# Chunk 0's keys in runs of 16 tokens, its lengths on GpSimd, its diagonal blocks from PSUM, and unread products moved into the joins

## The chip, the cores and the metric

The kernel runs on one core of a Trainium2 chip. The metric is the device time of one execution in microseconds. A core has five engines with instruction queues of their own: TensorE (PE for its products, PEld for its weight loads), VectorE (DVE), ScalarE (ACT), GpSimd (POOL) and SyncE (SP), which here only issues transfers. The tensors lie in HBM, the engines work in SBUF (128 partitions), and TensorE writes to the banks of PSUM.

## The reference

A delta-rule attention over 768 tokens for 4 x 8 heads of 48 channels, whose output goes through a feed-forward block with SiLU:

```python
q, k, v: (4, 8, 768, 48); beta: (4, 8, 768); w_in: (384, 2048); w_out: (2048, 384)
k_n = k / (np.linalg.norm(k, axis=-1, keepdims=True) + 1e-06)
for t in range(S):
    y[:, :, t] = np.einsum('bhd,bhde->bhe', q[:, :, t], state)
    v_old = np.einsum('bhde,bhd->bhe', state, kt)          # kt, vt, bt: token t
    state = state + bt[:, :, :, None] * np.einsum('bhd,bhe->bhde', kt, vt - v_old)
x = y.transpose(0, 2, 1, 3).reshape(B * S, H * D)
h = x @ w_in
out = (h * (1.0 / (1.0 + np.exp(-h)))) @ w_out
```

The keys are divided by their lengths. All is float32.

## The kernel before

The 768 tokens are six chunks of 128. Within a chunk the recurrence becomes algebra. The products of the chunk's keys with each other (the scores, `ap`) are scaled by a step for each token and head (minus beta over the square of the length), and a triangular matrix of 32 x 32 blocks is inverted: first the diagonal blocks, by a chain of small VectorE operations, then the blocks are joined by small TensorE products. The values times that inverse give `z`, and from `z` come the chunk's outputs and the update of the state. The outputs, turned into `xT`, run through the feed-forward block in half chunks.

Chunk 0 has nothing to hide behind, and the change concerns its opening. In the order of the program:

- `load_k(0)`: six transfers on SP bring the keys to `kbufs[0]` (`kb` in the profile), 48 floats of one token and head at a time, padded to 64. The padding is zeroed by VectorE. Beta comes by six transfers on ScalarE's queue, then the queries of chunk 0 (`z`'s buffer) on SP.
- `busy(n)` (L340 to L352) puts `n` products on TensorE whose result is never read, 384 wide: three at the start, four behind the first query turns, two behind the betas, six within the inversion.
- Lengths: GpSimd squares the keys (L385), VectorE adds (L389), and `norm_steps(0)` (L391 on) does the reciprocal square root by three rounds of small VectorE operations, then the step of each token and turns it (L426).
- `turn(0, b, 0, ...)` transposes the keys by TensorE (L510) and `first_score(b)` makes the scores of batch row `b` (L539), which ScalarE and VectorE copy to `ap`.
- `diagonal_blocks(0, g, ...)` copies the 32 x 32 blocks on the diagonal from `ap` to `stage`, eight copies by GpSimd and ScalarE, and `turn_diagonal(0)` (L578) turns them on VectorE.
- `invert_first` is the chain: scale by the step (L697), fifteen rounds of L705 and L709, two turns (L716, L720).
- `joins(0)` joins the blocks: `corner` (L743, its sums on VectorE at L750), `turned` (L759), `straight` (L772) and `merge_half` (L832), for each of two groups of batch rows (`g`). The list `between` says what is put behind each of the ten stages: `fill(1)` and `begin_next()` are steps that narrow the weights to the form that the feed-forward block uses (L233, L234 on ScalarE, L238, L242 on VectorE, L246 on GpSimd).
- Then `inner` (L866), `first_outputs` (L910), and the first feed-forward products (`phid`, L1088). From there a script of letters sets the order, with the second half of the chunk and the next chunks threaded between feed-forward products.

Each engine takes its instructions in program order (`pin` ties each to the one before). SP's transfers are in one line (`in_line`). Transfers of later weights are released by counts of TensorE instructions (`loads`): the first two, in `fetch_w_in(2)` and `(3)`, within `turned` and `straight`.

## Time and profile before

| | |
|---|---|
| median of 3 runs | 634.13 us (633.98 to 637.14) |
| the profiled execution | 633.96 us |
| its span in the profile | 631.8 us |
| TensorE busy | 617.7 us (98%) |
| VectorE / ScalarE / GpSimd busy | 415.5 / 226.7 / 94.0 us |
| mean granted TensorE clock over the span | 0.989 |

The profile is of one execution. Times in it count from the span's start; what lies around the span is 2.2 us. A row of the timeline gives start, length, engine, line, operation, output and input, and in brackets how long the engine had been idle and what ended that. A row of the groups ends with the busy time and the mean length in ns, then the idle time ahead of it. A row of a stretch gives its length and then, for PE, PEld, DVE, ACT and POOL, the busy time with the number of instructions, and last the granted clock, the share of the DMA engines and GB/s. "issue" is a wait for nothing that the profile shows.

### The profile page before, as it was taken

To read this page: it belongs to the slowest core of one execution; us is meant where nothing else is said; L and a number is where in the kernel's file an instruction comes from. 1 tells how busy PE (TensorE), PEld (TensorE's weight loads), DVE (VectorE), ACT (ScalarE), POOL (GpSimd) and SP (SyncE) were. 2 spreads that over 40 slices of the span, in tenths; PEclk is the share of its full clock that TensorE was granted. 3 is DMA by queue.
4 is the path that set the end of the run, shared out by engine and by line. 5 is a ranking of instruction groups with operands and counts; after the bars stand their busy time and mean duration, and the time that the engine had idled before them with its cause. 6 is when DMAs were issued, how large, how long until landed. Compare 5 with 4: busy or idle time off the path is not lost.

```text
span 631.8 us, 21374 instructions
## 1 busy us (share of the span) xinstructions
PE 617.7 (98%) x9390; PEld 543.3 (86%) x9390; DVE 415.5 (66%) x927; ACT 226.7 (36%) x516; POOL 94.0 (15%) x101
## 2 busy tenths in 40 slices
PE   8889989999999999999999999999999999999997
PEld 5578778666799989989989989989989989988997
DVE  6886779999667974546975554976444983345432
ACT  4657873332441122451122451122452122454210
POOL 5234631335020020020020010020002000000000
PEclk9869999999999999999999999999999999999999
DMA  9656506350459360459141359433254024010011
GB/s 175 134 141 199 170 16 149 116 86 4 101 100 186 62 108 4 95 107 188 34 92 20 72 125 156 65 75 44 52 113 95 2 75 62 17 38 1 0 26 26
DMA packets 136941, 52.61 MB, mean 83 GB/s; under 512 B 108672, under 2 KB 130432, under 8 KB 136848
## 3 DMA queue, kind: packets, MB, share of 16 engines
q1 hardware_dynamic: 136512, 51.09, 39.6%
q8 instruction: 74, 1.21, 0.9%
q10 hardware_dynamic: 336, 0.15, 0.1%
q14 instruction: 19, 0.16, 0.1%
HBM read 39.09 MB, written 9.96 MB: 78 GB/s over the span
## 4 chain that ended last, share of the span: by engine, by line
PE 93%; SPq 2%; DMA 1%; issue 1%; ACT 1%; DVE 0%
PE phid L1088 34%; PE px L1200 17%; PE py L1200 13%; PE po L1132 5%; PE pb_c L866 3%; PE pa L539 2%; SPq L144 2%; PE pb_c L1303 2%; PE pb_c L854 2%; PE pyc L945 2%; PE pc L1303 2%; PE pb_c L1132 2%; PE pb_c L886 2%; PE pa L1303 1%; PE pyc L932 1%; PE px L808 1%
## 5 line engine op out<-in xcount | busy, mean ns | idle before, releaser
L1088 PE MATMUL phid<-xT,w_in 128*128 128x256 f32 x960 | 214.9, 382 | 1.9 <-issue 1.7
L1088 PEld LDWEIGHTS phid<-xT,w_in 128*128 128x128 f32 x960 | 180.2, 190 | 26.9 <-issue 2.8
L1098 ACT ACTIVATE gT<-phid 128x512 f32<-128x512 f32 x72 | 42.9, 597 | 115.2 <-PE phid L1088 106.2
L656 DVE SCALAR_TENSOR_TENSOR rank<-g,step,x 128x31 f32<-128x31 f32 (+15 forms) x124 | 49.8, 402 | 23.3 <-DMA g<-blocks 19.8
L1200 PE MATMUL px<-sums_of_w,sums_of_g 128*128 128x192 f32 x320 | 56.6, 329 | 0.0
L1200 PE MATMUL py<-w_out,sums_of_g 128*128 128x192 f32 x320 | 56.2, 328 | 0.0
L1200 PEld LDWEIGHTS px<-sums_of_w,sums_of_g 128*128 128x128 f32 x320 | 52.2, 190 | 0.4
L1200 PEld LDWEIGHTS py<-w_out,sums_of_g 128*128 128x128 f32 x320 | 52.3, 190 | 0.3
L661 DVE TENSOR_TENSOR x<-x,rank 128x31 f32<-128x31 f32 (+15 forms) x124 | 42.5, 342 | 4.3
L477 POOL TENSOR_TENSOR vf<-vf,n_slot 128x768 f32<-128x768 f32 x10 | 14.8, 1492 | 175.4 <-DMA vf<-in_v_dram 129.9
L1183 DVE TENSOR_TENSOR sums_of_g<-gT 128x384 f32<-128x384 f32 (+1 forms) x48 | 24.6, 540 | 14.6 <-ACT gT L1098 14.5
L498 DVE STREAM_TRANSPOSE kq<-stage 128x512 f32<-128x512 f32 x28 | 28.4, 1121 | 6.8 <-DMA stage<-in_q_dram 3.5
L554 ACT COPY xT<-pyc 48x128 f32<-48x128 f32 (+2 forms) x120 | 31.1, 259 | 1.6
L1211 DVE TENSOR_TENSOR o<-o,kept 128x192 f32<-128x192 f32 (+1 forms) x29 | 11.5, 425 | 26.7 <-ACT kept L1208 26.7
L560 POOL COPY g<-x 64x256 f32<-64x256 f32 x4 | 5.0, 1244 | 150.8 <-DVE x L664 150.8
L891 DVE TENSOR_TENSOR state<-state,pb_c 128x384 f32<-128x384 f32 x22 | 11.2, 550 | 24.6 <-PE pb_c L886 24.6
L866 PEld LDWEIGHTS pb_c<-vf,xi 64*64 64x64 f32 x736 | 23.3, 138 | 3.2 <-issue 2.3
L866 PE MATMUL pb_c<-vf,xi 64*64 64x48 f32 x736 | 24.9, 223 | 0.1
L1132 PE MATMUL po<-w_out,gT 128*128 128x384 f32 x64 | 23.7, 491 | 0.0
L1200 PE MATMUL py<-w_out,gT 128*128 128x192 f32 x128 | 23.4, 331 | 0.0
L859 DVE TENSOR_TENSOR vf<-vf,pb_c 128x384 f32<-128x384 f32 x22 | 11.2, 550 | 18.3 <-PE pb_c L854 15.5
L1200 PE MATMUL px<-w_out,gT 128*128 128x192 f32 x128 | 22.4, 327 | 0.0
(293 smaller groups left out, 1094.5 us busy)
## 6 DMA issues: line engine op xcount, KB each, us to landing
vf<-in_v_dram SPq DMA_DIRECT2D x48, 96.0 KB, 2.8
out_dram<-o SPq DMA_DIRECT2D x42, 96.0 KB, 2.2
w_out<-in_moe_w_in_dram SPq DMA_DIRECT2D x4, 768.0 KB, 5.0
sums_of_w<-in_moe_w_out_dram SPq DMA_DIRECT2D x4, 768.0 KB, 4.6
kb<-in_k_dram SPq DMA_DIRECT2D x12, 192.0 KB, 4.5
kb<-in_k_dram SPq DMA_DIRECT2D x24, 96.0 KB, 4.0
raw<-in_moe_w_in_dram SPq DMA_DIRECT2D x3, 768.0 KB, 6.8
blocks<-ap SPq DMA_DIRECT2D x32, 64.0 KB, 1.9
```

Source lines behind the costliest of these rows:

```text
L477: pin(nc.gpsimd.tensor_tensor(out=vf, in0=vf, in1=of, op=ALU.mult))
L498: pin(nc.vector.transpose(out=kqs[c, b][:, :, j, :].rearrange("p a (i m) -> p a m i", i=T), in_=src.rearrange("p a (m d) -> p a m d", d=D) ...
L554: return pin(nc.scalar.copy(to, of))
L656: pin(nc.vector.scalar_tensor_tensor(out=tv, in0=g[:, 0:m, m : m + 1].to_broadcast([P, m, n]), scalar=step[:, m : m + 1], in1=x[:, m : m + ...
L661: yield pin(nc.vector.tensor_tensor(out=x[:, 0:m, m:T], in0=x[:, 0:m, m:T], in1=tv, op=ALU.add))
L866: yield pin(nc.tensor.matmul(pz[rows, n * D : (n + 1) * D], lhsT=xis[g][rows, u * H + 2 * p + e, :], rhs=vfs[c][rows, hf, g * HB + u, p, : ...
L1088: pin(nc.tensor.matmul(ph[:, j * GT : (j + 1) * GT], lhsT=w_in[:, a, (2 * f + j) * P : (2 * f + j + 1) * P], rhs=xTs[c, hf][:, a, :], star ...
L1098: pin(nc.scalar.activation(out=hidden_of(c, hf, f), in_=ph[:], func=ACTF.Silu, scale=-0.5 if in_blocks(c) else 0.5))
L1132: pin(nc.tensor.matmul(pos[i][:, 0:DM], lhsT=hidden_of(0, hf, f // 2)[:, at : at + C], rhs=w_outs[f // HFF][:, f % HFF, :], start=(f == 0) ...
L1183: pin(nc.vector.tensor_tensor(out=sums_of_g[:, k, fs], in0=of[0], in1=of[1], op=op))
L1200: pin(nc.tensor.matmul(to, lhsT=at, rhs=quarter(f, *b) if isinstance(b, tuple) else sums_of_w[b][:, f], start=start and f == 0, stop=f == ...
L1303: pin(nc.tensor.matmul(to[:, i * GT : (i + 1) * GT], lhsT=left(a, slice(f, f + 1))[:, 0], rhs=right(b), start=start and i == 0 and n == 0, ...
```

## The change

Chunk 0's keys come a second way. Two transfers bring them to `stage` (`keys_0`), for even and for odd heads; partition p holds 16 tokens in a row of one head, 3 KB in one piece. ScalarE and VectorE pad them into `kbufs[0]` (`pad`), TensorE turns them four steps at a time (`first_turn`), and a rearranged `turned_kq` takes them. The squares are made by ScalarE and GpSimd in two halves, the sums by VectorE; since tokens now lie along the free axis, four products with a selector matrix `sel` (built by VectorE from the identity) bring the sums to the tokens' partitions. GpSimd then does the reciprocal square root in fourteen small operations (`first_step`). The scores of a whole group stay in two PSUM banks; the diagonal blocks are taken from there by ScalarE and VectorE with the masks `halves`, and copied to `ap` afterwards. `load_k(0)` in its old form comes later, behind the values, for the update of the state. Half of beta's transfers move to SP. Unread products: three at the start with zeros as weights, then one 512 wide in two places, one 384 wide in two places within the inversion, and four 512 wide in the joins (`kept`).

```diff
-    for g in range(2):
-        load_k(0, slice(HB * g, HB * (g + 1)))
+    for e in range(2):
+        issue(
+            keys_0[:, e],
+            k.rearrange("b (a e) (c i s) d -> e c (b a) i (s d)", e=2, c=NCH, i=2 * NB)[e, 0],
+        )
...
+    def first_step():
+        po = bank(M, "po")
+        for i in range(2):
+            for e in range(2):
+                pin(nc.tensor.matmul(
+                    po[:, STEPS * i : STEPS * (i + 1)], lhsT=sel[:, e, i].rearrange("p j g n f -> p (j g n f)"),
+                    rhs=ss_0[:, e], start=e == 0, stop=e == 1,
+                ))
...
+        pin(nc.scalar.copy(ss, po[:, 0:T]))
+        pool, root = nc.gpsimd, seed.bitcast(FP32)
...
+        plus(n, u, None, 1e-6)
+        product(n_2, n, n)
+        yield
+        step_of[0] = small.tile([P, T], FP32, name="step")
+        pin(nc.vector.reciprocal(out=r, in_=n_2))
+        pin(nc.vector.scalar_tensor_tensor(
+            out=step_of[0][:], in0=r, scalar=-1.0, in1=stage[:, BH * T : BH * T + T], op0=ALU.mult, op1=ALU.mult
+        ))
+        pin(nc.scalar.copy(blocks[0][2].rearrange("p s t -> p (s t)")[:, 0 : T * T : T + 1], step_of[0][:]))
...
+    def first_score(g):
...
+        for e in range(2):
+            of = pa[e][:].rearrange("p (n t) -> p n t", t=W)
+            to = diagonals[0][:, HH * g + e : HH * (g + 1) : 2]
+            pin(nc.scalar.mul(to, of[:, :, 0:T], halves[:, 0:1]))
+            pin(nc.vector.scalar_tensor_tensor(
+                out=to, in0=of[:, :, T:W], scalar=halves[:, 1:2], in1=to, op0=ALU.mult, op1=ALU.add
+            ))
...
     load_v(0)
+    load_k(0)
     for b in range(2):
         turn(0, b, 1, M)
-    busy(4)
-    for _ in norm_steps(0):
-        pass
+    busy(1, wide=HB * NP * W)
+    next(steps)
...
-        if n in (9, 11, 13):
-            busy(2 if n < 13 else 1, done, Sync)
+        if n in (12, 14):
+            busy(1, done, Sync)
...
+    def kept():
+        busy(1, wide=HB * NP * W)
+
     together(joins(0, [
         lambda: (size_half(0, pins[seen_on]), begin_next(),),
-        lambda: (),
+        kept,
         lambda: (),
         lambda: (fill(1), fill(1),),
-        lambda: (fill(1),),
+        lambda: (fill(1), kept()),
         lambda: (),
-        lambda: (fill(1),),
-        lambda: (fill(1), begin_next(),),
+        lambda: (fill(1), kept()),
+        lambda: (fill(1), begin_next(), kept()),
```

On VectorE, around the turn of chunk 0's diagonals (`sums_of_w<-stage`), before: `n` and `nr`, `nt` are the lengths and what comes of them, `rank` the inversion's scratch.

```order
L417 TENSOR_TENSOR nt<-nr,ss 128x32
L418 TENSOR_SCALAR n<-nt 128x32
L419 RECIPROCAL nr<-n 128x32
L420 TENSOR_TENSOR nt<-nr,beta_tok 128x32
L423 SCALAR_TENSOR_TENSOR nt<-nr,nt 128x32
L426 STREAM_TRANSPOSE step<-nt 128x32
L578 STREAM_TRANSPOSE sums_of_w<-stage 128x32x32
L697 TENSOR_TENSOR sums_of_w<-sums_of_w,step 128x2x16x16
```

On VectorE at the same place, now: `pa` and `pb_c` are the PSUM banks with the scores.

```order
L447 TENSOR_REDUCE ss<-sq 128x2x8 x2
L1622 STREAM_TRANSPOSE stage<-beta_tok 128x32
L1597 SCALAR_TENSOR_TENSOR stage<-pa_232,halves,stage 128x8x32
L1597 SCALAR_TENSOR_TENSOR stage<-pb_c_73,halves,stage 128x8x32
L1597 SCALAR_TENSOR_TENSOR stage<-pa_271,halves,stage 128x8x32
L1597 SCALAR_TENSOR_TENSOR stage<-pb_c_74,halves,stage 128x8x32
L712 STREAM_TRANSPOSE sums_of_w<-stage 128x32x32
L508 RECIPROCAL nr<-seed 128x32
L509 SCALAR_TENSOR_TENSOR step<-nr,stage 128x32
L831 TENSOR_TENSOR sums_of_w<-sums_of_w,step 128x2x16x16
```

The root's sixteen steps have left VectorE; the diagonals come from PSUM in four steps, and the reciprocal and the step stand behind the turn.

On TensorE, from the second chunk's key turns (`pt<-ident,kb`) within the inversion to the first corner products (`ap`), before: `pb_c<-state,ident` are unread products.

```order
L347 MATMUL pb_c_74<-state_90,ident 128x384
L347 MATMUL pb_c_75<-state_90,ident 128x384
L510 MATMUL pt<-ident,kb_77 128x128 x4
L347 MATMUL pb_c_73<-state_90,ident 128x384
L347 MATMUL pb_c_74<-state_90,ident 128x384
L743 MATMUL pl<-sums_of_w,ap_168 32x16 x2
```

On TensorE at the same place, now, and then the end of the corners with the start of `turned` (L893):

```order
L643 MATMUL pt<-ident,kb_77 128x128 x12
L376 MATMUL pb_c_75<-state_96,ident 128x384
L643 MATMUL pt<-ident,kb_77 128x128 x4
L376 MATMUL pb_c_73<-state_96,ident 128x384
L877 MATMUL pl<-sums_of_w,ap_230 32x16 x2
...
L877 MATMUL pl<-sums_of_w,ap_269 32x16 x2
L376 MATMUL pb_c_73<-state_96,ident 128x512
L893 MATMUL pl<-sums_of_w 32x32
```

Of six unread products within the inversion two are left, and the first of the four kept ones stands between the corners and `turned`.

On SP, from the values (`vf`) to the queries of chunk 1 (`sums_of_g`), before: `w_out` takes raw parts of `moe_w_in`.

```order
L292 DMA raw<-in_moe_w_in_dram 128x3x512
L198 DMA vf<-in_v_dram 64x8x48 x8
L292 DMA w_out_109<-in_moe_w_in_dram 128x3x512 x2
L144 DMA sums_of_g<-in_q_dram 128x8x48
L144 DMA sums_of_g<-in_q_dram 64x8x48 x2
```

On SP at the same place, now:

```order
L303 DMA raw<-in_moe_w_in_dram 128x3x512
L198 DMA vf<-in_v_dram 64x8x48 x8
L144 DMA kb_76<-in_k_dram 128x8x48
L144 DMA kb_76<-in_k_dram 64x8x48 x2
L144 DMA kb_76<-in_k_dram 128x8x48
L144 DMA kb_76<-in_k_dram 64x8x48 x2
L303 DMA w_out_115<-in_moe_w_in_dram 128x3x512 x2
```

The six transfers of chunk 0's keys, which stood first on SP, now stand between the values and the next weights.

More of the change, by code (lines that the diff above doesn't have):

```diff
@@ L314 @@
     pin(nc.gpsimd.memset(states[0][:], 0.0))
+    zeros = states[0][:].rearrange("p u a w -> p (u a w)")
+    for _ in range(3):
+        done = pin(nc.tensor.matmul(
+            bank(CC, "pw")[:, 0:DM], lhsT=zeros[:, 0:P], rhs=zeros[:, 0:DM], start=True, stop=True
+        ))
+        tensor.append(done.ins.engine)
     make_identity(nc, ident[:])
@@ L1483 @@
     load_v(0)
+    load_k(0)
     for b in range(2):
         turn(0, b, 1, M)
[L1486 to L1488 removed]
+    busy(1, wide=HB * NP * W)
+    next(steps)
     first_queries(0)
```

189 lines of the change are left out of this document (144 added, 45 removed).

## The prediction

> **What bounds the kernel now.** First the page, for TensorE's share, then the busy time of each engine by stage: from 16.5 us (the lengths end on VectorE) to 31.2 (the joins begin), to 49.3 (the first product of the feed-forward), and the long rest from 92.
>
> ```profile
> PE 617.7 (98%) x9390; PEld 543.3 (86%) x9390; DVE 415.5 (66%) x927; ACT 226.7 (36%) x516; POOL 94.0 (15%) x101
> ...
> q8 instruction: 74, 1.21, 0.9%
> ...
> 16.50:31.20 14.70, 13.01 (x177) 8.77 (x179) 13.20 (x35) 9.28 (x24) 2.93 (x6) 0.88 0.69 138
> 31.20:49.30 18.10, 15.53 (x721) 14.61 (x721) 14.23 (x28) 10.20 (x22) 6.42 (x4) 0.72 0.53 135
> ...
> 92.00:631.80 539.80, 535.54 (x7240) 477.57 (x7240) 346.76 (x765) 165.00 (x391) 53.61 (x47) 1.00 0.37 73
> ```
>
> After each stage's length stand the busy times of PE, PEld, DVE, ACT and POOL with their counts, then TensorE's granted clock. From 92 us TensorE works 535.54 of 539.80 us; the change touches nothing there. So its worth is how much earlier the first feed-forward product (49.31) comes. Ahead of it PE's busy share flatters: much of it is unread products, and from 31.2 to 49.3 the clock is 0.72, which makes some 10 of the 18.1 us run at half.
>
> The opening hangs on one chain, seen in the order of time on VectorE, with ScalarE's and SP's rows that feed it:
>
> ```profile
> 2.65 0.48 DVE L208 MEMSET sums_of_g<- 128x512 f32 x1
> 15.45 0.35 DVE L419 RECIPROCAL nr<-n 128x32 f32<-128x32 f32 x1
> 16.18 0.19 DVE L423 SCALAR_TENSOR_TENSOR nt<-nr,nt 128x32 f32<-128x32 f32 x1
> 16.40 0.21 DVE L426 STREAM_TRANSPOSE step<-nt 128x32 f32<-128x32 f32 x1
> 16.54 1.98 DVE L578 STREAM_TRANSPOSE sums_of_w<-stage 128x1024 f32<-128x1024 f32 x1
> 18.55 0.69 DVE L697 TENSOR_TENSOR sums_of_w<-sums_of_w,step 128x512 f32<-128x512 f32 x1
> 28.01 1.06 DVE L716 STREAM_TRANSPOSE sums_of_w<-sums_of_w 128x512 f32<-128x512 f32 x1
> 28.92 1.95 DVE L720 STREAM_TRANSPOSE sums_of_w<-sums_of_w 128x1024 f32<-128x1024 f32 x1
> 31.92 0.34 DVE L750 SCALAR_TENSOR_TENSOR sums_of_w<-pl,second,pick 64x128 f32<-64x128 f32 x1 [1.05 <-PE pb_c L743]
> 12.30 3.75 ACT L554 COPY stage<-ap 32x512 f32<-32x512 f32 x6
> 6.23 1.61 POOL L385 TENSOR_TENSOR sq<-kb 128x384 f32<-128x384 f32 x2 [1.95 <-DMA kb<-in_k_dram]
> 9.00 1.61 POOL L385 TENSOR_TENSOR sq<-kb 128x384 f32<-128x384 f32 x2 [1.15 <-DMA kb<-in_k_dram]
> 33.12 4.36 SPq L292 DMA_DIRECT2D w_out<-in_moe_w_in_dram  x2
> 49.31 0.45 PE L1088 MATMUL phid<-xT,w_in 128*128 128x256 f32 x1 [0.15 <-DVE xT L919]
> ```
>
> The second half of the keys arrives at 9.00. The turn of the diagonals (L578, 16.54) then waits for two things that end together: the lengths on VectorE (their last step, L426, ends at 16.61) and ScalarE's copies of the diagonals (12.30 to 16.05). From there VectorE runs without a gap to 30.87, and then waits 1.05 us for the corners (L743).
>
> **Term 1, the turn of the diagonals comes earlier.** The rows for its parts:
>
> ```profile
> 1.00:2.00 1.00, 0.00 (x0) 0.00 (x0) 0.99 (x4) 0.00 (x0) 0.97 (x4) 1.00 0.10 27
> 13.00:14.00 1.00, 1.00 (x4) 0.57 (x3) 0.86 (x5) 0.99 (x2) 0.00 (x0) 1.00 1.01 369
> 16.72:17.92 1.20, 1.20 (x65) 1.13 (x66) 1.20 (x1) 0.89 (x3) 1.17 (x3) 1.00 0.92 162
> 9.12 1.06 PE L510 MATMUL pt<-ident,kb 128*128 128x128 f32 x8
> L522 DVE COPY kq<-pt 128x512 f32<-128x512 f32 x2 | 1.4, 686 | 0.2 <-PE pt L510 0.2
> L557 DVE COPY z<-pb_c 128x384 f32<-128x384 f32 x1 | 0.6, 560 | 0.0
> L389 DVE TENSOR_REDUCE ss<-sq 128x8 f32<-128x384 f32 x4 | 2.2, 545 | 2.6 <-POOL sq L385 2.6
> L557 DVE COPY ap<-pb_c 128x256 f32<-128x256 f32 x4 | 1.7, 425 | 0.5 <-PE pb_c L539 0.4
> L554 ACT COPY ap<-pa 128x256 f32<-128x256 f32 x8 | 3.0, 378 | 1.0 <-PE pb_c L539 0.8
> L1493 POOL COPY sums_of_w<-step 128x32 f32<-128x32 f32 x1 | 0.2, 249 | 0.1
> L1496 POOL MEMSET xi<- 128x1024 f32 x2 | 1.8, 955 | 0.0
> ```
>
> Keys: 0.786 MB in 3 KB runs. Bytes start to flow near 1.9 us; the weights, in 2 KB runs, flow at 369 GB/s in the second row, against 162 in the third, where 192-byte rows move. So 1.9 + 0.786/0.369 = 4.0 us at best, 6.8 at 162 GB/s, 9.0 as now. VectorE comes to the padding behind its memsets (over at 3.1, as now) and the 12 small copies that build the selector (at 0.19, as L423): 5.4; copies this small may follow each other closer, so I start the padding at 5.3. Two copies of 384 by VectorE, 2 x 0.5: 6.3. A small reduction (0.2) and a key copy (0.69): 7.2. Two sums of 768, each twice 0.545: 9.4; the squares on GpSimd (1.61 from 6.3) hide under that, and so do the transposes (0.53 for four). The four selector products and ScalarE's copy 0.6: 10.0. TensorE does 32 score products in 1.2 us (65 records in the third row), two groups: 12.4. After the last group ScalarE scales twice (2 x 0.38), VectorE adds behind it (0.42): 13.6. So the turn starts at **13.6 instead of 16.54**, -2.9; bounds 12.7 (keys and selector early) to 15.6 (keys at 6.8, half a us more in the copies).
>
> Lengths on GpSimd: its squares end near 8, three memsets of 0.95 follow, 10.8; then 14 small operations at 0.25 (the 128x32 copy; bounds 0.2 and 0.4, half a 384 product): 14.3, by bounds 13.6 to 16.4. They are needed when the turn is done, 13.6 + 2.0 = 15.6. Covered by 1.3 us, short by 0.8 at the upper bound.
>
> Behind the turn VectorE now does the reciprocal and the step (0.35 + 0.19, with gaps 0.65), and ahead of the corner sums one small transpose (0.21). The 16 steps are unchanged, 18.55 to 30.87. So the corner sums could start at 13.6 + 1.98 + 0.65 + 12.32 + 0.21 = 28.8, against 31.92: **-3.1**. The corner products must keep up. Now they do not:
>
> ```profile
> 28.21 1.29 PE pb_c L347 x4
> 31.16 0.20 PE L743 MATMUL pl<-sums_of_w,ap 32*32 32x16 f32 x2
> ```
>
> The corners' operand is turned at 29.07 (L716), yet they start at 31.16: the line that stands ahead of them on TensorE is the unread product (1.29 us for two, 0.645 each). The new order leaves two there instead of six, so the corners are ready in time, if the clock holds.
>
> **Term 2, joins to first product.** From 31.92 to 49.31 are 17.39 us, 10 of them at half clock. TensorE's waits and its instruction counts name a second limit:
>
> ```profile
> 32.49:35.90 3.41, 2.15 (x133) 1.81 (x132) 2.91 (x8) 1.45 (x4) 1.48 (x1) 0.98 0.44 108
> 35.90:39.31 3.41, 2.43 (x127) 2.29 (x128) 3.26 (x7) 1.88 (x5) 1.83 (x1) 0.50 0.59 178
> PE px L832 <- issue: 1.1, 1, 1.1
> PE py L832 <- issue: 1.1, 1, 1.1
> 35.92:39.48 3.56, 2.43 (x127) 2.29 (x128) 3.41 (x7) 2.04 (x5) 1.83 (x1) 0.50 0.62 183
> 35.93:49.31 13.38, 12.09 (x459) 11.51 (x460) 10.76 (x20) 7.69 (x16) 3.74 (x2) 0.62 0.60 154
> ```
>
> TensorE stops twice for 1.1 us with nothing to wait for, before 35.93 and before 39.49, and between the two restarts lie 127 + 128 = 255 instructions. All its 18780 instructions over the 74 packets (1.21 MB) of its instruction queue q8 give 254 each. So I read the stops as waits for the next packet: at best 256 instructions per 3.56 us here. From 35.93 to 49.31 are 919 instructions, 3.6 packets, 12.8 us if supply alone counts. Full clock can therefore gain little: 13.38 - 12.4 (three packets, 10.7, then the last products and two copies of 0.5, near 1.7) = 1.0. The four kept products (512 wide: 512/384 of 0.645 is 0.86 each, 3.4 together) fall into the same waits and I cost them at nothing; uncovered they cost 3.4. **-1.0**, bounds -2.7 (supply no limit) and +2.4.
>
> [...]
>
> **Moved transfers.** Six key transfers now stand between the values and the next weights on SP. SP idled from 26.30 to 33.12 there. Values end some 2 us earlier; six issues take 4.9 us at the values' rate (6.51 for eight) and 7.5 at the second keys', so SP is free between 29 and 32, and the weights' turn comes near 30. Cost 0; at the long end they come 2 us late, ScalarE's narrowing waits, and the last two join copies behind it.
>
> ```profile
> 19.79 6.51 SPq L198 DMA_DIRECT2D vf<-in_v_dram  x8
> 10.64 7.50 SPq L144 DMA_DIRECT2D kb<-in_k_dram  x6
> ```
>
> **Sum.** -3.1 - 1.0 = -4.1 on the profiled execution's 633.96: 629.9. The median shown is 634.13, 0.17 above it; I forecast **629.9**.
>
> **Rivals.** *Half clock from the corners on* (slower). The clock halved at 35.9 after a stretch in which TensorE was busy 2.15 of 3.41 us with 32-row products. Fifteen unread products ran ahead of the joins; now seven do, three of them before 4 us. If the clock falls before the corners, near 27 us, what ran at full clock from 31.16 to 35.9 (some 3.5 us of work) takes 3.5 longer, less the first stop of 1.1: +2.4; the kept products take 1.7 each, 6.9, and hide only under the two stops, 2.2: +4.7. Corners to first product: 18.15 + 7.1 = 25.2; the corners start at 27.5, so the product comes at 52.7, 3.4 late: **637.4**. It decides if no full clock returns before the inner products (L866). Against it: a kept product drives 128 rows, a join product 32. Chance 0.08.
>
> *One stretch at half clock*, within the joins, after which the kept products restore it: kept products and joins cost 1.9 more: **631.8**. Chance 0.2. [...]
>
> *The opening does not get earlier*: the runs land hardly sooner, or the lengths on GpSimd end at 16.4 and beyond. Term 1 shrinks to -1.1: **631.9**. For it: GpSimd's chain has 1.3 us of cover only. Chance 0.22.
>
> [...] Chance 0.1.
>
> **How the numbers follow.** The forecast has 0.40. What a measurement of this kernel can tell is about 0.5%, 3.2 us: faster is below 631.0, slower above 637.3. Faster: nearly all of the forecast (0.36) and of the fourth rival (0.1), and a quarter of the second and third (0.11): 0.57. Slower: the first rival and a little for a delay behind the moved transfers: 0.09. Within: 0.34. Range: from 627.2 (turn at 12.7 and term 2 near -2.7, less likely together) to 634.4 (turn at 15.6 and one stretch at half clock, or late weights); above it stays the slower rival, 0.1 on each side.
>
> **What would show it.** Right: the turn of the diagonals (L712) near 13.6, the first corner sum (L884) near 28.8 with no wait for TensorE, the first product near 45.2, granted clock 1.0 from there back to the corners, and issue stops some 256 instructions apart. Wrong: VectorE waiting for GpSimd at the reciprocal (L508), padding that starts after 6.5, clock 0.5 at the corners, or ScalarE waiting for weights (L244) in the joins.

## The result and the profile after

The changed kernel takes 639.38 us (median of 20 runs, 634.87 to 643.17) against 634.12 us (20 runs, 632.29 to 637.72) for the kernel before on the same chip: a ratio of 1.0076, 95% interval 1.0057 to 1.0096. Forecast was 629.9, range 627.2 to 634.4. It is 5 us slower, not 4 faster. The profiled execution took 639.39 us, its span is 637.7 us against 631.8.

The page's busy times hardly moved. The clock row, which is in tenths for 40 equal slices, even rose in the second and third slice (here after, and the last line before):

```profile
PE 620.9 (97%) x9390; PEld 543.6 (85%) x9390; DVE 414.2 (65%) x932; ACT 228.8 (36%) x520; POOL 95.4 (15%) x111
...
PEclk9999999999999999999999999999999999999999
...
PEclk9869999999999999999999999999999999999999
```

The timeline has the milestones: the turn of the diagonals, the first corner sum, the first feed-forward product; and the chain of waits has the long run of 96 such products, here after and then before.

```profile
19.54 1.97 DVE L712 STREAM_TRANSPOSE sums_of_w<-stage 128x1024 f32<-128x1024 f32 x1
34.95 0.34 DVE L884 SCALAR_TENSOR_TENSOR sums_of_w<-pl,second,pick 64x128 f32<-64x128 f32 x1 [0.64 <-PE pb_c L877]
52.47 0.70 PE L1222 MATMUL phid<-xT,w_in 128*128 128x256 f32 x2
97.27 20.92 PE phid L1222 x96
```

```profile
91.96 20.92 PE phid L1088 x96
```

The first three stood at 16.54, 31.92 and 49.31. So the span's 5.9 us are: 3.0 until the corner sum (34.95 against 31.92), 0.1 in the joins (17.52 us from there to the first product, 17.39 before), 2.2 from there to the 96 products (44.80 against 42.65), and 0.6 behind them, which I did not follow.

**Where the first 3.0 us are.** The groups of TensorE's opening, by line and shape, up to 20 us: busy time, then mean ns of one.

```profile
L328 PE MATMUL pb_c<-state 128*128 128x384 f32 x6 | 4.2, 874 | 1.4 <-POOL state L325 1.4
L455 PE MATMUL pt<-ident,kb 128*128 128x128 f32 x16 | 3.9, 423 | 2.6 <-DVE kb L691 2.2 <-DVE kq L691 0.4
L1591 PE MATMUL pa<-kq 48*64 48x64 f32 x64 | 3.7, 313 | 0.0
```

A score product is modelled at 313 ns. Before (L539) it is 222:

```profile
L539 PE MATMUL pa<-kq 48*64 48x64 f32 x96 | 3.5, 222 | 1.2 <-ACT kq L520 1.2
```

The longer durations are those of half clock, though the stretch from 0 to 16.5 us prints 1.00 for the granted clock: the trace has no step of the clock until 20.4 us (before: 8.4), that step is one up to full, and where none is recorded yet a row says 1.00. The same products show it in the kernel before, where they last 0.31 us ahead of the step at 8.43 us and 0.22 us behind it; e1 below has them at 220 ns with the clock up, and e17 at 313 ns with half clock recorded from 12.1 to 18.9 us. TensorE works on its three unread products, then idles 2.2 us for the padded keys (L455's wait on L691), and the clock stays down through transposes and scores. It falls once more from 30.6 to 34.0 us, under the corners.

**Where the 2.2 us are.** TensorE's waits from 49 to 70 us. Before, the only row there is a wait of 0.2 on VectorE (the first line here); now there are two for "issue":

```profile
PE phid L1088 <- DVE xT L919: 0.2, 1, 0.2
...
PE pb_c L966 <- issue: 1.4, 1, 1.4
PE pl L893 <- issue: 1.0, 1, 1.0
```

TensorE stops twice, at 55.3 and 60.3 us, at the 2216th and the 2472nd of its records (products and weight loads, counted together in order of time), 256 apart: instructions that have not come. I read them as arriving in packets of 256, by transfers of their own: the page counts 74 transfers and 1.21 MB on the instruction queue q8, 254 of TensorE's 18780 records to each. In 20 of the 28 cases of the table under e17 such a transfer (a fetch) begins 0.7 to 1.4 us after TensorE enters a packet. Here the fetches that belong to the entries at 51.68 and 56.29 us begin at 53.85 and 59.39, 2.2 and 3.1 us later. SP had issued a 768 KB transfer of weights ahead of each, at 51.55 and 55.33 (the fifth and sixth part of `moe_w_in`, weights 4 and 5 below). The packets of weights 4 move from 52.5 to 55.6 us and those of weights 5 from 56.0 to 59.3, so the first fetch begins amid them and the second at their end; the trace doesn't say which transfer engine held which.

```profile
51.55 0.37 SPq L303 DMA_DIRECT2D w_out<-in_moe_w_in_dram  x1
55.33 0.37 SPq L303 DMA_DIRECT2D w_out<-in_moe_w_in_dram  x1
```

Before, the same two issues come 0.22 and 0.25 us behind the entries (48.19, 51.89), and the fetches begin at 49.08 and 52.88:

```profile
48.41 0.37 SPq L292 DMA_DIRECT2D w_out<-in_moe_w_in_dram  x1
52.14 0.37 SPq L292 DMA_DIRECT2D w_out<-in_moe_w_in_dram  x1
```

From this reading come the theories: a cold opening; unread products in the joins that cost what they bring; fetches behind weights. The rival to all three is that the time is set elsewhere and these are signs only.

### The profile page after: what moved, and what is told of

The parts are those of the page before. It is cut to its first block, busy times and chain, and to the rows that moved or that the text cites. A ratio compares the mean times of both kernels' runs of the same rounds, so it can differ in the third digit from the quotient of the medians.

```text
span 637.7 us, 21390 instructions
## 1 busy us (share of the span) xinstructions
PE 620.9 (97%) x9390; PEld 543.6 (85%) x9390; DVE 414.2 (65%) x932; ACT 228.8 (36%) x520; POOL 95.4 (15%) x111
## 3 DMA queue, kind: packets, MB, share of 16 engines
q8 instruction: 74, 1.21, 0.8%
## 4 chain that ended last, share of the span: by engine, by line
PE 95%; DVE 1%; ACT 1%; issue 1%; DMA 1%; SPq 0%; DVEq 0%; ACTq 0%
PE phid L1222 33%; PE px L1334 17%; PE py L1334 13%; PE po L1266 5%; PE pa L672 2%; PE pb_c L1000 2%; PE pb_c L1437 2%; PE pb_c L988 2%; PE pyc L1079 2%; PE pc L1437 2%; PE pb_c L1266 2%; PE pb_c L1020 2%; PE pa L1437 1%; PE pb_c L376 1%; PE pyc L1066 1%
## 5 line engine op out<-in xcount | busy, mean ns | idle before, releaser
L993 DVE TENSOR_TENSOR vf<-vf,pb_c 128x384 f32<-128x384 f32 x22 | 11.2, 550 | 18.2 <-PE pb_c L988 18.1
```

## The experiments

Ratios are to the kernel before, run on the same chip with each batch.

### The opening

**e1_warm5.** Five opening products, so that TensorE is busy until the keys come.

```diff
-    for _ in range(3):
+    for _ in range(5):
         done = pin(nc.tensor.matmul(
             bank(CC, "pw")[:, 0:DM], lhsT=zeros[:, 0:P], rhs=zeros[:, 0:DM], start=True, stop=True
```

> The changed kernel with five instead of three unread products at the start, so that TensorE is busy until the first keys are turned. Theory A (TensorE runs at half clock from the start until it has been busy for some time; the gap of 2.2 us before the key transposes keeps it there until 20 us): the score products take 2.4 us for 64 instead of 3.7 and the diagonals are turned 1.5 to 2.5 us earlier (17 to 18 instead of 19.5); time 2 to 2.5 us below the changed kernel, about 637. Rival B (the gap does not set the clock; the opening is late because the keys land at 7.3 and the copies are slow): the products at most delay the transposes, time 0 to +0.6 us.

The same groups and milestones:

```profile
L455 PE MATMUL pt<-ident,kb 128*128 128x128 f32 x16 | 2.1, 276 | 2.2 <-DVE kb L691 1.4 <-DVE kq L691 0.8
L1591 PE MATMUL pa<-kq 48*64 48x64 f32 x64 | 2.1, 220 | 0.0
16.17 1.96 DVE L712 STREAM_TRANSPOSE sums_of_w<-stage 128x1024 f32<-128x1024 f32 x1
31.86 0.34 DVE L884 SCALAR_TENSOR_TENSOR sums_of_w<-pl,second,pick 64x128 f32<-64x128 f32 x1 [0.92 <-PE pb_c L877]
```

The clock rises at 4.5 us, transposes fall from 423 to 276 ns, scores from 313 to 220, and the diagonals are turned 3.4 us earlier. That part of theory A is shown. Its time is not: 639.97 us, ratio 1.0114 (1.0090 to 1.0138), no better than the changed kernel's 1.0076. The gain is lost behind the joins:

```profile
PE pl L893 <- issue: 1.8, 1, 1.8
PE phid L1222 <- DMA xT<-part: 1.6, 1, 1.6
```

The first is the stop for instructions again, longer, and half clock follows it (55.7 to 59.1). The second, at 97.9 us, is new: the two products add eight instructions, and every packet boundary behind them falls elsewhere in the program.

**e4_before_cold.** The opposite: the kernel before made cold.

```diff
-    busy(3)
+    busy(3, wide=8)
```

> The kernel before with its three opening unread products shrunk to 8 columns, so that TensorE idles until the first keys are turned. Theory A (clock at half until TensorE has been busy for a while): the transposes and score products of the opening take nearly twice as long (score products 0.31 instead of 0.22 us), the diagonals are turned 1 to 2 us later than 16.5, time +1 to +2 us on the kernel before. Rival B: no effect, 0.

635.17 us, ratio 1.0029 (1.0012 to 1.0045), +1.8 us by the ratio: theory A. The size is right and part of the working is not: the clock rose at 10.1 us, only 1.7 later than before, so scores took 237 ns on average and the diagonals were turned at 17.19, 0.65 later. The other half of the delay at the first feed-forward product (50.59 against 49.31) arises in the joins. Why the clock came up so soon here, and not until 20.4 in the changed kernel, is not shown; gaps in TensorE's work alone don't explain it, since the changed kernel has none from 13.55 to 16.97 us and stays at half.

**e8_keys_alone.** On e5_warm_late (below), the step sizes' transfers come behind the keys.

```diff
     load_q(0, slice(0, HB))
+    betas(0, False)      # three, on SP, taken from ahead of this line
     load_q(0, slice(HB, B))
...
     padded = [pad(h) for h in range(2)]
+    betas(1, True)       # three, on ScalarE
```

> The version with both repairs, and the step sizes' small transfers issued behind the keys: three of them on ScalarE after its padding, three on SP after half of the queries. Theory A (these small packets delay the keys, which land at 5.2 and 7.3 us): the odd heads land by 6.3. Rival B (the two key transfers take that long by themselves): 7.3 again within 0.3.

VectorE's padding of the odd heads, which waits for the keys, in the changed kernel and then here:

```profile
7.30 0.63 DVE L691 COPY kb<-stage 128x384 f32<-128x384 f32 x2 [2.95 <-DMA stage<-in_k_dram]
```

```profile
6.75 0.63 DVE L694 COPY kb<-stage 128x384 f32<-128x384 f32 x2 [2.40 <-DMA stage<-in_k_dram]
```

0.55 us (0.59 against e5, whose row starts at 7.34), between the two theories: the small transfers are a quarter of the 2.0 us by which the keys miss the forecast's 5.3. It was run once (637.52 us), so its time tells nothing. With the rest the two key transfers move 0.79 MB from 1.9 to 6.7 us, 164 GB/s, the lower end that the prediction gave.

### The joins

**e2_no_kept.** The four unread products of the joins are left out.

```diff
     def kept():
-        busy(1, wide=HB * NP * W)
+        pass
```

> The changed kernel without the unread products in the joins (the counts that release the weights are lowered to suit). Theory A (each of them stands 1.05 us in the chain of the joins; the instruction supply does not hide them): the joins to the first feed-forward product take 1 to 3 us less than 17.6, time 1 to 3 us below the changed kernel. Theory B (they hold the clock): half clock for some 10 us of the joins as in the kernel before, joins as long or up to 3 us longer, time 0 to +3.

638.06 us, ratio 1.0079 (1.0059 to 1.0100), the changed kernel's. The clock is half from 40.9 to 51.1 us, so the products do hold it (theory B), and the joins last 18.4 us. But sixteen instructions fewer move the boundaries too, and a wait for xT of 1.9 us is new, as in e1. So the comparison was made again with the count kept:

**e11_late_keys0 and e12_no_kept_same_count.** Both are built on e10_wide_late_betas (below), with the second load of chunk 0's keys later; e12 moves the four products out of the joins, 8 columns wide, to the start.

```diff
-    load_k(0)
...
+        (WINDOW + PACKET * 7 + 100, load_k, 0),
         (WINDOW + PACKET * 8 + 45, fetch_w_in, 6),
```

> The same, and chunk 0's second load of keys (0.79 MB in 192-byte rows), which the change put behind the values at 26.6 to 30.5 us, released between weights 5 and 6 instead. Theory A (in the old place it holds up the instruction fetch at 31): that fetch comes near 29, no stop at 32, first product of the feed-forward near 47, time 1.5 to 2 us lower, at or below the kernel before. Rival B (the fetch waits for something else): the stop stays, time the same; if the new place collides with weight 6 or the fetches after 55 us, up to +1.

> The same without the four unread products in the joins; four of 8 columns at the start keep the count of instructions. Theory A (what they cost in the chain, 1.05 us each, and what the full clock returns are equal): half clock for some 10 us of the joins, time the same within 0.7. Rival B (the prediction: they cost nothing and full clock gives 1.0): +1 us or more. Rival C (they cost more than they return): -1 us or more.

e11: 637.91 us, ratio 1.0054 (1.0034 to 1.0074), 3 us worse than e10. The fetch that I suspected behind the moved keys came at 30.8 (30.9 in e10), so the transfer did not hold it up; its new place brought stops of 0.8 and 1.3 us at 61.7 and 70.6. Theory A is refuted. e12: 636.52, 1.0033 (1.0016 to 1.0050). The stretch from 34 to 50 us, after its length the five engines' busy times, and behind them the clock, with the products in the joins (e11) and without (e12):

```profile
34.00:50.00 16.00, 13.88 (x568) 10.58 (x562) 13.21 (x24) 9.48 (x20) 5.29 (x4) 1.00 0.60 152
```

```profile
34.00:50.00 16.00, 13.28 (x509) 12.59 (x505) 12.13 (x22) 8.31 (x18) 4.62 (x3) 0.57 0.61 152
```

With clock 1.00 or 0.57 the way from the first corner sum to the first feed-forward product takes 18.35 or 18.63 us (31.56 to 49.91, 32.25 to 50.88). In time e12 is 1.4 us ahead, which by the medians is rival C, but the intervals overlap and theory A is not excluded. Rival B, the prediction's price, is: e12 should have lost 1 us. The four products give back what they take, or a little less.

**e6_warm_late_kept256.** On e5_warm_late, these products half as wide.

```diff
-        busy(1, wide=HB * NP * W)
+        busy(1, wide=HB * NP * W // 2)
```

> The same with the four unread products of the joins 256 instead of 512 wide. Theory A (they lie in the chain of the joins at 1.05 us each and half the width holds the clock as well): joins 1 to 2 us shorter, time 1 to 2 us below the version with 512. Rival B (the supply of instructions, 256 in 3.6 to 3.9 us, sets the joins at full clock): joins the same within 0.5. Rival C (half the width no longer holds the clock): half clock in the joins, 0 to +2 us.

637.35 us, ratio 1.0065 (1.0042 to 1.0088), against 636.91 and 1.0064 with 512. Clock half from 38.8 to 49.0: rival C. Half the width does not hold the clock in that execution, whose joins take 19.9 us against 18.0 in e5's; in time nothing of that can be measured.

### The fetches and the weights

**e3_late_weights.** Three weight transfers 60 instructions later.

```diff
-        (WINDOW + PACKET * 6 + -15, fetch_w_in, 4),
-        (WINDOW + PACKET * 7 + -15, fetch_w_in, 5),
-        (WINDOW + PACKET * 8 + -15, fetch_w_in, 6),
+        (WINDOW + PACKET * 6 + 45, fetch_w_in, 4),
+        (WINDOW + PACKET * 7 + 45, fetch_w_in, 5),
+        (WINDOW + PACKET * 8 + 45, fetch_w_in, 6),
```

> The changed kernel with the three weight transfers 4, 5 and 6 released 60 instructions later. Theory A (these transfers get ahead of the fetch of the next instructions, which makes the two stops of 1.0 and 1.4 us at 55 and 60 us): both stops vanish, time 2 us lower. Rival B (the stops come from the fetches themselves, which are late since the joins use instructions as fast as they come): the stops stay, time the same within 0.5.

Both stops are gone: TensorE's waits from 50 to 66 us are a single row again.

```profile
PE phid L1222 <- DVE xT L1053: 0.2, 1, 0.2
```

The two fetches begin 1.1 us behind their entries instead of 2.2 and 3.1. That is theory A for the stops: the early weights made them. The time, 636.67 us, ratio 1.0068 (1.0049 to 1.0087), is not 2 us better than 1.0076 within what this measures.

**e5_warm_late**, both repairs, with five opening products.

```diff
-    for _ in range(3):
+    for _ in range(5):
...
-        (WINDOW + PACKET * 6 + -15, fetch_w_in, 4),
+        (WINDOW + PACKET * 6 + 45, fetch_w_in, 4),
```

(5 and 6 likewise.)

> The changed kernel with both repairs: five unread products at the start, and weights 4, 5 and 6 released 60 instructions later. Theory A (the loss is the cold clock of the opening, 3.1 us, and the instruction fetches that queue behind weights, 2.5 us): the diagonals are turned at 16.2, the corners start at 31.1, no stop at 55 or 60 us, the first product of the feed-forward near 49; time 5 us below the changed kernel, within 1 us of the kernel before. Rival B (the time is set later, by the supply of instructions or transfers, whatever the opening does): 1 us or less below the changed kernel.

636.91 us, ratio 1.0064 (1.0045 to 1.0082). No stop at 55 or 60, but the wait for xT of 1.2 us is there, as in e1, e6 and e8, which have the same eight instructions more. By the time that is rival B. The milestones are theory A's (diagonals at 16.18, no stops, first product at 49.95), in an execution of 634.78, the lowest of the six. Most of the gain was still missing.

**e9_wide_late.** The opening warmed without a change in the count, by wider products, and the late weights of e3.

```diff
-            bank(CC, "pw")[:, 0:DM], lhsT=zeros[:, 0:P], rhs=zeros[:, 0:DM], start=True, stop=True
+            bank(CC, "pw")[:, 0:HB * NP * W], lhsT=zeros[:, 0:P], rhs=zeros[:, 0:HB * NP * W], start=True, stop=True
```

> The changed kernel with its three opening unread products 512 instead of 384 wide, and weights 4 to 6 released 60 instructions later; the count of instructions stays that of the changed kernel, where the version with five products has eight more and showed a new stop of 1.2 us at 94 us, for a transfer of xT. Theory A (the eight instructions shift the fetches against the transfers): no stop at 94, corners at 31.1 to 31.4, no stops at 55 and 60; 1 to 1.5 us below the version with five products. Rival B (the stop is chance): same as that version within 0.5. If 5.6 us of opening products are too short for the clock in some executions, the spread of the runs is wide and the median 1 us higher.

635.82 us, ratio 1.0018 (1.0003 to 1.0034). Theory A: no wait for xT, none of the two stops, and 0.6% better than the changed kernel with intervals far apart (from e16, the changed kernel's second batch, 0.4%, and there the intervals overlap a little). The turn and the corners come within 0.5 us of e1's, then the long stretch that takes 42.7 us as before:

```profile
16.58 1.98 DVE L712 STREAM_TRANSPOSE sums_of_w<-stage 128x1024 f32<-128x1024 f32 x1
32.36 0.34 DVE L884 SCALAR_TENSOR_TENSOR sums_of_w<-pl,second,pick 64x128 f32<-64x128 f32 x1 [0.97 <-PE pb_c L877]
50.32 0.89 PE L1222 MATMUL phid<-xT,w_in 128*128 128x256 f32 x3
50.30:93.00 42.70, 41.09 (x1093) 33.76 (x1092) 30.97 (x67) 33.92 (x67) 21.55 (x16) 1.00 0.44 137
```

**e10_wide_late_betas**, with the step sizes behind the keys (the diff of e8) on e9.

> The same, and the step sizes' small transfers behind the keys. Theory A (the chain from the keys sets the corners): keys 0.55 us earlier, corners at 29.6 to 30.5, time 0.5 us lower. Rival B (the fetch of the packet that begins at the 946th instruction comes at 31.0, behind the moved keys of chunk 0, and sets what follows): corners earlier, a stop of 1.6 us at 32.3, time the same.

634.98 us, ratio 1.0010 (0.9994 to 1.0026): level with the kernel before. The diagonals are turned at 15.86 and the corner sum is at 31.39, 1.0 earlier than in e9, yet the first product comes at 50.37 against 50.32. The stop of rival B is not at 32.3, but TensorE stops 1.05 us at the 1202nd record (36.5) and 1.03 at the 1800th (46.1): what the corners gain, the supply of instructions takes.

**e13_wide and e17_wide_again.** The wide opening products alone, on the changed kernel (the diff of e9 and nothing else).

> The changed kernel with its three opening unread products 512 instead of 384 wide, nothing else, and the same count of instructions. With late weights besides, the ratio to the kernel before was 1.0018, late weights alone gave 1.0068, the changed kernel 1.0076. Theory A (the two losses add: cold opening about 3 us, fetches behind weights about 2): ratio 1.004 to 1.005, the stops at about 52 and 57 us stay. Theory B (they overlap; each repair only pays with the other): ratio 1.006 or more.

> The version with 512 wide opening products and nothing else once more, for a profile: its profile was of the lowest of six executions, 634.62, the others lay between 637.8 and 640.7 at a lower granted clock. Theory A (a longer stop at 55 to 58 us for an instruction fetch idles TensorE and the clock falls behind it): stops of 2 us or more together there, half clock within 5 us of them. Rival B: the stops are as in the first profile (1.1 us) and the time goes elsewhere, in the joins.

e13: 638.54 us, ratio 1.0093 (1.0061 to 1.0125): theory B, a warm opening pays only with the late weights. Its profile is of the fastest of its six executions; e17 shows one of 641.09, and in it theory A of that run: one stop, and TensorE's clock behind it (0.66 from 54 to 64 us; by the recorded steps half from 56.5 to 63.3):

```profile
PE pl L893 <- issue: 2.6, 1, 2.6
54.00:64.00 10.00, 7.37 (x152) 5.72 (x144) 3.10 (x7) 3.78 (x7) 0.95 (x1) 0.66 0.30 91
```

From the 1966th to the 2727th record TensorE takes 17.9 us there, 14.3 in e13's own profile, 15.2 in the changed kernel's, 12.6 before and 12.5 in e9. In this execution the late fetch cost its own wait, and half clock followed.

e17's opening was not warm all through either: the clock rose at 5.3 us, was half again from 12.1 to 18.9, the scores took 313 ns as in the changed kernel, and the turn came at 17.93 (16.57 in e13). So it goes in seven of the eleven profiles with a mended opening (e8 to e11, e13, e15, e17): the clock falls between 11.8 and 14.3 us for 3.4 or 6.8 us, and the turn comes between 15.9 and 17.9. More or wider products at the start brought the clock up (at 4.5 us in e1, at 5.3 in e17), but in these seven it did not hold through what followed.

The issue of weights 4 and 5 on SP against TensorE's entry into the packet of its 1966th and 2216th record, behind which the next fetch goes, for all pairs within 1 us of each other in all profiles, from the traces' records:

| kernel, weights | issue minus entry, us | fetch after entry, us |
|---|---|---|
| before, 4 and 5 | +0.22, +0.25 | 0.9, 1.0 |
| e4, 4 and 5 | +0.22, +0.25 | 0.9, 0.7 |
| e2, 4 and 5 | +0.16, +0.12 | 0.7, 0.8 |
| nine kernels with late weights, 4 | +0.47 to +0.48 | 0.9 to 1.2 |
| e13, 4 | +0.22 | 1.1 |
| e14, 4 | +0.10 | 1.4 |
| e18, 4 and 5 | +0.04, -0.30 | 0.8, 1.0 |
| e7, 4 and 5 | +0.01, +0.22 | 1.4, 2.5 |
| changed, 4 and 5 | -0.13, -0.96 | 2.2, 3.1 |
| e1, 4 | -0.26 | 3.0 |
| e13, 5 | -0.08 | 2.7 |
| e14, 5 | -0.69 | 3.5 |
| e16, 4 | -0.32 | 4.0 |
| e17, 4 | -0.39 | 4.0 |

Weights issued ahead of the entry go with a fetch 2 us and more behind it in seven of eight cases; issued after it, in one of twenty. The release of weights 4 hangs on an instruction a little ahead of the boundary. Where TensorE had caught up with its supply it halted at the boundary itself (0.2 us in the changed kernel, 0.3 in e1, 0.4 in e16 and in e17, none in e13), and the weights passed it. With the late release the fetch at the 2472nd record comes 2.3 us behind its entry instead, where TensorE does not stop for it.

**e18_before_early.** The collision put into the kernel before: the same three transfers 45 instructions earlier.

```diff
-        (WINDOW + PACKET * 6 + -15, fetch_w_in, 4),
+        (WINDOW + PACKET * 6 + -60, fetch_w_in, 4),
```

(5 and 6 likewise.)

> The kernel before with weights 4, 5 and 6 released 45 instructions earlier, nothing else: the suspected cost put into the kernel that doesn't have it. Theory A (a weight transfer that starts ahead of an instruction fetch holds it up, and TensorE with it): stops of 1 us or more at the 2216th or 2472nd instruction (52 to 58 us), time +1.5 to +4 us, ratio 1.002 to 1.006. Rival B (the fetches came late in the changed kernel for another reason): no new stop, ratio 1.000 within 0.002.

635.30 us, ratio 1.0019 (1.0003 to 1.0034). The profile has no new stop: weights 4 were issued 0.04 us behind the entry, since SP's queries ended at 46.24 and this issue follows them by 0.92 as it does in the kernel before (0.90), and weights 5, 0.30 ahead, did not get in front. The loss of 1.1 us is at the edge of what this tells, and its place was not in the profiled execution. Inconclusive: the edit did not make the collision it was meant to make, so that early weights delay a fetch rests on e3, which takes them away, and on the table.

### The halves

**e7_before_kept and e14_opening_only.** The second half of the change on the kernel before, and the first half alone.

```diff
 (e7, on the kernel before)
-        if n in (9, 11, 13):
-            busy(2 if n < 13 else 1, done, Sync)
+        if n in (12, 14):
+            busy(1, done, Sync)
...
-        if n == 14:
-            busy(1, done, Sync)
... and kept() in the joins as in the changed kernel
 (e14, on the changed kernel: the same lines back, and kept() empty)
```

> The kernel before with the second half of the change alone: the unread products of the inversion and the four 512 wide ones of the joins stand as in the changed kernel, the opening is the old one. Theory A (the parts add up; the joins gain nothing since each of these products costs what the full clock returns): corners up to 0.8 us earlier than 31.16, joins at full clock but no shorter than 17.4 by over 0.5, time between -1 and +0.5 us on the kernel before; if fetches queue behind weights at 52 and 56 us as in the changed kernel, +1.5. Rival B (the prediction's term 2): first feed-forward product 1 us earlier from the joins alone, time -1.5 to -2.

> The changed kernel's opening with the unread products of the inversion and of the joins where the kernel before has them: the first half of the change alone. The second half alone gave 1.0033. Theory A (the halves add): ratio 1.004 to 1.005, diagonals turned at 19.5, half clock in the joins. Theory B (the halves hurt each other: the fetches meet the weights only when the joins run at full clock): ratio 1.002 or less, no stops at 55 and 60. The prediction's term 1 alone would give 0.995.

e7: 634.07 us, ratio 1.0033 (1.0008 to 1.0058). In its profiled execution (633.26) the corner sum comes 1.3 us earlier, at 30.59, the joins run at clock 1.00, and take 17.8 us to the first product (48.38), 0.4 more than before at 0.72. Rival B, the prediction's term, is refuted again; theory A holds for the joins, and the time, +2.1 us by the ratio, is nearer to its case of late fetches (+1.5; the second fetch came 2.5 us behind its entry). Its executions fall in two groups: seven of twelve with a mean clock of 0.996 to 0.999 take 632.0 to 634.9, the other five at 0.986 to 0.991 take 635.7 to 638.4. No profile shows where the clock falls in the second group.

e14: 635.97, 1.0054 (1.0031 to 1.0078). Diagonals at 19.87, half clock in the joins, 17.6 us long; and the stops are there, 0.7 and 2.0. So theory B is refuted: they do not need a joins stretch at full clock. The halves cost 0.3% and 0.5%, the whole 0.6 to 0.8%: they add, within the intervals.

**e15_opening_mended.** e14 with e10's opening and late weights.

> The same with the mended opening (512 wide products, step sizes behind the keys) and late weights: the best guess at a version ahead of both. Theory A (the four products in the joins cost a little more than the full clock returns): corners near 30.7, ratio 0.998 to 1.000. Theory B (they pay for themselves): ratio 1.001 to 1.003.

634.69 us, ratio 1.0016 (0.9992 to 1.0039), 630.27 to 636.54. Neither theory is told from the other, and it is not ahead of the kernel before. In its profile the turn comes at 17.86, and a stop for instructions of 1.8 us that ends at 86.2 is followed by half clock from 86.9 to 90.3; the kernel before stops there for 1.7 us and runs at full behind it.

**e16_after_again.** The changed kernel a second time.

> The changed kernel once more, for a second profile at another phase of the clock's steps. Theory A (whether the clock rises in the opening hangs on how the 4.2 us of opening products lie to steps of 3.4 us): the clock rises either near 8 us or near 20 us, the diagonals are turned at 17 or at 19.5, and the time follows by 2 to 3 us. Rival B: the opening is the same in every execution.

636.08 us, ratio 1.0058 (1.0031 to 1.0085), which agrees with 1.0076. The opening is as cold as the first time (first step of the clock at 20.4 us, diagonals at 19.72): rival B for the turn, which stands between 19.5 and 19.9 in all five profiles with this opening. The clock is not alike in all five: in e14 it was up from 4.2 to 7.6 us, when TensorE worked 0.8 us in all, and half again until 21.3. What differs from the first profile is one stop:

```profile
PE pl L893 <- issue: 2.6, 1, 2.6
```

## Why the prediction was wrong

Where the 10 us between forecast and measurement are, by the profiles: 5.9 in the turn of the diagonals, 0.2 from there to the corner sum, 1.1 in the joins and 2.7 behind the first feed-forward product.

**Term 1 failed in its durations.** The turn came at 19.5, not 13.6. All its rows were read where TensorE ran at full clock, or in the opening of before, whose unread products run into the transposes without a gap. The step that failed is "TensorE does 32 score products in 1.2 us ..., two groups: 12.4": 64 took 3.7 us, 18.1 was their end, and the transposes, "0.53 for four", took 0.98. With the clock up (e1, e9) the turn stands at 16.2 to 16.6: half of the 6 us error is the clock, shown. The rest I read from rows and did not isolate, but for 0.55: the keys, at 7.3 instead of 5.3, where VectorE had waited 2.95 us for them (0.55 of it the step sizes, e8); the four selector products, 1.9 us, and 1.1 with the clock up, where 0.6 was counted with the copy behind them; and strided key copies, 1.03 us instead of the 0.69 taken from the old layout,

```profile
8.93 1.03 DVE L691 COPY kq<-pt 128x512 f32<-128x512 f32 x1 [0.92 <-PE pt L455]
```

The prediction named the padding after 6.5 as a sign of failure; it was one. GpSimd's lengths were no limit, as forecast: VectorE does not wait for them.

Here 4.2 us of products, an idle 2.2 us and small products left the clock half until 20.4 us; 5 us and more of products with shorter gaps raised it at 4.4 to 7.5 (e1, e5, e9). The steps in all these traces lie 3.41 us or multiples of it apart (10.24, 3.41, 13.65 and 10.24 us between the first five of the kernel before). The forecast took its opening at full clock from rows of the kernel before, so a half-clock opening belonged among the rivals.

**Term 2 failed at "fall into the same waits and I cost them at nothing".** The joins split at TensorE's restart behind its first stop for instructions: 35.93 us before, 40.03 in the changed kernel.

```profile
31.92:35.93 4.01, 2.72 (x197) 2.39 (x184) 3.48 (x9) 1.80 (x5) 1.96 (x2) 0.98 0.39 96
34.95:40.03 5.08, 4.64 (x202) 2.96 (x191) 4.01 (x10) 1.90 (x5) 3.20 (x5) 1.00 0.32 90
40.03:52.47 12.44, 11.36 (x460) 8.88 (x460) 10.12 (x19) 7.45 (x16) 3.75 (x2) 1.00 0.63 158
```

Behind the restart it takes 12.4 us, as forecast, and partly by luck: three packets took 11.6, not 10.7, and the rest 0.8, not 1.7. Ahead of it, where both kernels run at full clock, it takes 5.1 instead of 4.0. Two of the four kept products stand there, and the stop that was to take them up shrank only from 1.13 to 0.44. Three of the four kept products in the changed kernel:

```profile
35.44 1.13 PE L376 MATMUL pb_c<-state,ident 128*128 128x512 f32 x2
38.22 1.13 PE L376 MATMUL pb_c<-state,ident 128*128 128x512 f32 x2
41.11 1.13 PE L376 MATMUL pb_c<-state,ident 128*128 128x512 f32 x2
```

They do hold the clock, at 1.00 in the joins (0.57 without them, e12). They stand ahead of the join products in TensorE's order, and the term is +0.1 instead of -1.0. Over all twenty profiles the way from corner sum to first product takes 17.0 to 20.3 us at a clock of 0.63 to 1.00, and the length does not follow the clock (16.98 us at 0.80 in e15, 20.27 at 0.83 in e8). That the supply of instructions sets it fits and is not shown alone. No run shows the -2.7, supply no limit, which stands as the term's lower bound, in the low end of the range and in the fourth rival's 0.1: the shortest way in the twenty profiles, e15's 16.98 us, is 0.4 below the 17.39 of before. The upper bound of +2.4 held the term. (The range's upper end, 634.4, does not come out of its own terms: 629.9 with 2.0 for the turn and 1.9 for one stretch at half clock is 633.8.)

**"the change touches nothing there" failed**, the sentence on the stretch behind 92 us and, unsaid, on the one from 49.3. The program there is the same, but the weights' releases are counts of instructions. Before, they put the issues of weights 4 and 5 at 0.22 and 0.25 us behind TensorE's entries into the packets; in the changed kernel, where TensorE arrives short of instructions, they stand 0.13 and 0.96 us ahead of them. From the 1966th to the 2727th record the changed kernel took 15.2 us in its first profile and 16.7 in its second (e16) against 12.6 before. To arrive late is not needed for this: e1 and e13, on time at the corners, have stops too. No rival had it. The moved key transfers cost nothing that shows: SP was done with them at 30.5, 6.5 us ahead of the next weights, the fetch behind them did not move when they were taken away (e11), and ScalarE did not wait for weights in the joins. (The values did not end 2 us earlier, as the prediction has it, but at 26.5 against 26.3.)

**The slow rival** gave 637.4, near the time, for the wrong reason. The clock was half under the corners (30.6 to 34.0 us), as it said, but the joins ran at full (1.00). The late weights at the range's end were weights 2 and 3; what cost time were weights 4 and 5, and they came too early.

What stays open: of the changed kernel's 0.76% the warm opening, the later weights and the step sizes together take 0.66, and I do not know why the gain of the opening beyond that, 0.7 us at the turn of the diagonals in e10, reaches no further than the corners; nor what halves the clock in some executions of e7. Against the changed kernel's second batch (0.58%) the same three take 0.48. The turn at 13.6 was reached by no version, so what it would be worth is open.

## What to carry to other kernels

Read durations from the same clock that the new code will meet: the changed opening ran at half clock to 20.4 us, while the clock row printed 1.00 until the first recorded step. Here TensorE's instructions came at 256 per 3.6 us (before, between its two stops in the joins) to 3.9 us (the changed kernel, behind its restart), and their fetches began 2.2 to 4.0 us behind the entries in seven of the eight cases where weights were issued 0.1 to 1 us ahead of them. A shift of the work ahead brought two stops (1.0 and 1.4 us, the changed kernel), a shift of the number of instructions new waits (1.6 us in e1, 1.9 in e2): where releases are tuned to such a rate, tune them again behind either, and test it with the count held fixed.

## What the hardware showed unexpectedly

Products of 48 rows and 64 columns, 3.7 us of them in a row (14.4 to 18.1 in the changed kernel), did not raise the clock from half; it rose at 20.4. From 13.55 to 16.97 us TensorE had no gap at all, with these products in most of it (the row prints 1.00 since no step is recorded yet):

```profile
13.55:16.97 3.42, 3.42 (x101) 3.32 (x104) 0.26 (x2) 0.94 (x4) 1.94 (x8) 1.00 1.21 269
```

With a transfer of 768 KB issued 0.1 to 1 us ahead of TensorE's entry into a packet, the instruction fetch behind that entry began 2.2 to 4.0 us behind the entry instead of 0.7 to 1.4, in seven of eight cases, and releasing three such transfers later brought it back to 1.1 (e3). TensorE, idle for 1.8 to 2.6 us behind such a fetch, was then granted half clock for 3.4 to 6.8 us (e1, e14, e16, e17); behind stops of 1.0 and 1.4 us it was not (the changed kernel). Eight more instructions at the start brought a wait of 1.2 to 1.6 us at 94 to 98 us in four kernels, for a transfer of xT; an instruction fetch had begun 0.9 us ahead of each.
